# Attention over channels with a gated FFN on one core: k's norms spread by transposes and DMAs, and a new order for scalings, G/H tiles and one load of v

## The chip, the cores and the metric

The kernel runs on one core of a Trainium2 chip. TensorE multiplies matrices, VectorE, ScalarE and GpSimd work on elements, SyncE (SP) only issues DMAs. The metric is the time of one execution in microseconds on the device, the median of several runs; lower is better.

## The reference

```python
B, N, C = (4, 6016, 256)

def _attn_ref(q, k, v, tau):
    qn = q / (np.linalg.norm(q, axis=1, keepdims=True) + 1e-06)
    kn = k / (np.linalg.norm(k, axis=1, keepdims=True) + 1e-06)
    s = kn.transpose(0, 2, 1) @ qn / tau
    s = s - s.max(-1, keepdims=True)
    a = np.exp(s)
    a /= a.sum(-1, keepdims=True) + 1e-09
    return (v @ a).astype(np.float32)

def _moe_ref(x, w_gate, w_val, w_out):       # 24064 tokens, 256 -> 1536 -> 256
    gate = 1.0 / (1.0 + np.exp(-(x @ w_gate)))
    val = x @ w_val
    return (gate * val @ w_out).astype(np.float32)
```

The result is `_moe_ref` of the attention output, its four batches put one after another, with tau 1.0. q and k are normalised over the rows, one norm for each of the 256 channels, so the attention matrix is only 256 x 256 for each batch.

## The kernel before

**The algebra.** Since the attention output is v times a 256 x 256 matrix a, the kernel never forms it. For each batch it makes G = a w_gate and H = a w_val (256 x 1536 each, from the exponentials `e`, the weights and the row sums), and the GLU then works on v directly: `ps_gate` from G and the transposed v (`vT`), `ps_val` from H and vT. ScalarE takes tanh of half the gate (L518), VectorE forms (tanh + 1) times val in `hT` (L519). The output product with w_out is done as seven products of half-size blocks, for which VectorE makes operand sums of hT (`a_sum`, L541) and GpSimd, once, sums of w_out (`w_sums`, L215); sums of the products are put together by ScalarE copies (L595, L602) and GpSimd additions (L596 to L613).

**The tiling.** A batch has 47 row tiles of 128, in 12 chunks: eleven of four tiles and one of three (`NCH`, `groups`). A chunk has 12 slots, f = 0 to 11, one for each 128 of the 1536 hidden channels (`glu(b, ci, f)`). So a batch has 144 slots, numbered here from 0; slot 108 is chunk 9, f = 0. In each slot the order of the program is: the GLU block (two ps_gate and two ps_val matmuls), a twelfth of the output products of the chunk before (`run_work`), perhaps an operand sum, and then the side work listed for that slot. Operand sums come at f = 1, 3, 4, 5, 6 for the chunk before (`NEXT_SLOTS`) and at f = 7 to 11 for the chunk itself (`OWN_SLOTS`); f = 0 and 2 have none. The order on each engine is that of the program, written out by hand.

**Side work.** `side_work(b)` (L749 to L806) prepares batch n = b + 1 while batch b's GLU runs. It spreads over the first 96 slots the loads of q and k, the scores (`ps_s`, in the one-bank pool `pss`) and the squares for the norms. With s0 = 98 it then lists: the folding of the squares, the norm matmuls, an inverse root (GpSimd, L355 to L359) giving the four columns `r` for q and k, their reciprocals on VectorE at slot 108 (`norms_inv`), `spread_both` at slot 110, `copy_rk` at 111, the two scalings of the scores at 112 (`scale_x`, VectorE), the exponentials at 113 and 114 (`exps`, ScalarE), the row sums at 116 (`all_sums`), and the twelve G/H tiles (`gh`) at 117 + 9 i // 4, from 117 to 141, in turn in `pss` and in the other one-bank pool, `psm`. A tile with row block 0 is stored by ScalarE (L464), one with row block 1 by VectorE (L466).

**k's norms.** A scaling needs the q norm of a channel on each partition, which `r` has, and k's norms along the free axis on every partition, which it has not. `spread_both` makes this with TensorE: two fp32 matmuls of a broadcast column of `r` with the identity give `ps_rk` in PSUM, and ScalarE copies it to `rk_sb`. Batch 0 uses `spread_k` and `weights` instead, ahead of the GLU. `sums_start` opens the row-sum bank with a matmul of one row of ones with a row of eps (L413), and `row_sums` adds the sums of e to it.

**Queues.** GpSimd issues all loads of q, k, v and the weights[...]; at the start it issues batch 0's q and k, v's chunk 0, the weights of G and H in four pieces each (256, 256, 512, 512 columns), v's chunk 1, and w_out. Later v loads go two chunks ahead, at f = 0. SP issues the transpose of each v chunk (`transpose_v`, L483, listed at f = 2 of the chunk before; batch 0's chunk 0 goes through TensorE instead) and the stores of the output (L654, listed at f = 4). A DMA on SP waits for its data, and all behind it on SP wait with it.

Of the kernel before, what the change touches and what calls it, by code (L numbers as in the profile page):

```python
# [9 lines left out]
FP32 = mybir.dt.float32  # L10
BF16 = mybir.dt.bfloat16
# [42 lines left out]
def kernel(  # L54
# [20 lines left out]
    nc = tc.nc  # L75
    P = nc.NUM_PARTITIONS
# [4 lines left out]
    B, N, C = q.shape  # L81
    CW, DFF = moe_w_gate.shape
    assert CW == C and C % P == 0 and N % P == 0 and DFF % P == 0
    NT = N // P
    CB = C // P
    FC = DFF // P
# [4 lines left out]
    NCH = (NT + TPC - 1) // TPC  # L91
# [5 lines left out]
    def rows(x, b):  # L97
        return x[b].rearrange("(p t) c -> p t c", p=P)
# [3 lines left out]
    def pool(name, bufs, **kw):  # L102
        return ctx.enter_context(tc.tile_pool(name=name, bufs=bufs, **kw))

    consts = pool("consts", 1)
# [3 lines left out]
    attp = pool("attp", 1)  # L109
# [5 lines left out]
    spool = pool("spool", 1)  # L115
    mpool = pool("mpool", 2)
    opool = pool("opool", 2)
    psg = pool("psg", 2, space=PSUM)
    psv = pool("psv", 2, space=PSUM)
    pso = pool("pso", 2, space=PSUM)  # L120
    pss = pool("pss", 1, space=PSUM)
    psm = pool("psm", 1, space=PSUM)
# [3 lines left out]
    def mm(out, lhsT, rhs, start, stop, **kw):  # L126
        nc.tensor.matmul(out, lhsT=lhsT, rhs=rhs, start=start, stop=stop, **kw)  # L127
# [16 lines left out]
    def load_v(b, ci):  # L144
        t0, nt = groups[ci]
        v_sb = vpool.tile([P, TPC, C], BF16, tag="v", name="v_sb")
        nc.gpsimd.dma_start(out=v_sb[:, :nt, :], in_=rows(v, b)[:, t0 : t0 + nt, :])
        vs[b, ci] = v_sb
# [16 lines left out]
    ident_f = consts.tile([P, P], FP32)  # L165
    make_identity(nc, ident_f)
    ones_bf = consts.tile([P, P], BF16)
# [3 lines left out]
    one_two = consts.tile([P, 2], BF16)  # L171
    nc.vector.memset(one_two[:, 0:1], 1.0)
    nc.vector.memset(one_two[:, 1:2], 2.0)
    ones_row = consts.tile([1, P], BF16)
    nc.vector.memset(ones_row, 1.0)
    eps_row = consts.tile([1, CB, 2], BF16)
    nc.vector.memset(eps_row[:, :, 0:1], 1e-9)
    nc.vector.memset(eps_row[:, :, 1:2], 2e-9)
    shift = consts.tile([P, 1], FP32)
    nc.vector.memset(shift, -inv_tau)  # L180

# [8 lines left out]
    w_out_sb = consts.tile([P, FC, C], BF16)  # L190
    pieces = [(0, FG // 2), (FG // 2, FG // 2)] + [(fg * FG, FG) for fg in range(1, NFG)]
    for f0, nf in pieces:
        for w, src in enumerate((moe_w_gate, moe_w_val)):
            nc.gpsimd.dma_start(  # L194
                out=w_sb[w][f0 // FG][:, :, ds(f0 % FG, nf)],
                in_=src.rearrange("(t p) f -> p t f", p=P)[:, :, ds(f0, nf)],
            )
    load_v(0, 1)

    w_sums = consts.tile([P, len(B_SUMS), FC // 2, P], BF16)  # L200
    w_f32 = {}
# [1 line left out]
    for n in range(FC // TPC):  # L203
        w_f32[n] = f32pool.tile([P, TPC, C], FP32, tag="f32", name="w_f32")
        nc.gpsimd.dma_start(
            out=w_f32[n], in_=moe_w_out.rearrange("(t p) c -> p t c", p=P)[:, n * TPC : (n + 1) * TPC, :]
# [16 lines left out]
    st = {}  # L223
# [85 lines left out]
        )  # L309

    def spread_both(b):
        s = st[b]
        s["rk_ps"] = psm.tile([P, C], FP32, tag="m", name="ps_rk")
        for i in range(CB):
            mm(
                s["rk_ps"][:, ds(i * P, P)],
                s["r"][:, CB + i : CB + i + 1].to_broadcast([P, P]),
                ident_f,
                True,
                True,  # L320
            )

    def copy_rk(b):
        s = st[b]
        s["rk_sb"] = attp.tile([P, C], FP32, tag="rk", name="rk_sb")
        nc.scalar.copy(s["rk_sb"], s["rk_ps"])

    def norms_sqrt(b):
        s = st[b]
# [18 lines left out]
    def root_steps(b):  # L348

        s = st[b]  # L350
        x, y = s["sq_n"], s["y"]
        t = attp.tile([P, 2 * CB], FP32, tag="tn", name="t_n")
        s["r"] = attp.tile([P, 2 * CB], FP32, tag="r", name="r")
        for _ in range(3):
            nc.gpsimd.tensor_tensor(out=t, in0=x, in1=y, op=ALU.mult)  # L355
            nc.gpsimd.tensor_tensor(out=t, in0=t, in1=y, op=ALU.mult)
            nc.gpsimd.tensor_scalar(out=t, in0=t, scalar1=-0.5, scalar2=1.5, op0=ALU.mult, op1=ALU.add)
            nc.gpsimd.tensor_tensor(out=y, in0=y, in1=t, op=ALU.mult)
        nc.gpsimd.tensor_tensor(out=s["r"], in0=x, in1=y, op=ALU.mult)  # L359
# [50 lines left out]
    def sums_start(b, ni, pl, tag):  # L410

        ps_r = pl.tile([P, ni, 2], FP32, tag=tag, name="ps_r")
        mm(ps_r, ones_row, eps_row[:, :ni, :], start=True, stop=False, skip_group_check=True)  # L413
        return ps_r

    def row_sums(b, i0, ps_r):
# [224 lines left out]
    def run_work(work, share):  # L641

        upto = sum(w[0] for w in work) * share
        done = 0
        while work and done < upto:
            cost, fn, *args = work.pop(0)
            fn(*args)
            done += cost

    def store():  # L650
        while stores:
            b, ci = stores.pop(0)
            t0, nt = groups[ci]
            nc.sync.dma_start(out=out_rows[b][:, t0 : t0 + nt, :], in_=ffn.pop((b, ci))[:, :nt, :])  # L654
# [91 lines left out]
    gh(0, gh_first[3], pso, "o")  # L746


    def side_work(b):  # L749


        side = {}

        def at(slot, fn, *a):
            side.setdefault(divmod(slot, FC), []).append((fn, a))

        for ci in range(NCH):
            nb, nci = (b, ci + 1) if ci + 1 < NCH else (b + 1, 0)
            lb, lci = (b, ci + 2) if ci + 2 < NCH else (b + 1, ci + 2 - NCH)
            if nb < B:  # L760
                at(ci * FC + 2, transpose_v, nb, nci)
            if lb < B:
                at(ci * FC + 0, load_v, lb, lci)
            if (b, ci) == (0, 0):
                for i in range(FC // TPC):
                    at(8, copy_w_out, i)
                for n, m in enumerate((1, 0, 3, 2, 4)):
                    for i in range(FC // TPC):
                        at(10 + 2 * n, sum_w_out, m, i)
        n = b + 1  # L770
        if n == B:
            return side
        first, last = (14 if b == 0 else 0), 8 * FC
        for g, (t0, nt) in enumerate(groups):
            s0 = first + g * (last - first) // NCH
            if b == 0:
                at(max(0, s0 - 12), load_qk, n, t0, nt)
            elif s0 >= 24:
                at(s0 - 24, load_qk, n, t0, nt)
            for u in range(nt):  # L780
                at(first + (t0 + u) * (last - first) // NT, score, n, t0, u)
            if g == 0:
                at(s0, acc_start, n)
            for i, (fn, w) in enumerate(((acc_square, 0), (acc_add, 0), (acc_square, 1), (acc_add, 1))):
                at(s0 + 1 + 2 * i, fn, n, g, w)
        if n + 1 < B:
            for g, (t0, nt) in enumerate(groups[:3]):
                at(NCH * FC - 24 + 8 * g, load_qk, n + 1, t0, nt)
        s0 = 8 * FC + 2
        at(s0 if b == 0 else s0 - 2, acc_fold, n, 0)  # L790
        at(s0 + 1 if b == 0 else s0, acc_fold, n, 1)
        at(s0 + 3, norms_mm, n)
        at(s0 + 4, root_seed, n)
        at(s0 + 4, root_steps, n)
        at(s0 + 10, norms_inv, n)
        at(s0 + 12, spread_both, n)
        at(s0 + 13, copy_rk, n)
        at(s0 + 14, scale_x, n, 0)
        at(s0 + 14, scale_x, n, 1)
        at(s0 + 15, exps, n, 0)  # L800
        at(s0 + 16, exps, n, 1)
        at(s0 + 18, all_sums, n)
        at(s0 + 18, gh_tiles, n)
        for i, piece in enumerate(gh_order):
            at(s0 + 19 + 9 * i // 4, gh, n, piece, *((pss, "s"), (psm, "m"))[i % 2])
        return side  # L806


# [5 lines left out]
    def gh_piece(n):  # L814
        gh(0, gh_first[n], *gh_banks[n % 4])

    prev = None
    for b in range(B):
        side = side_work(b)
        for ci in range(NCH):  # L820
            final = (b, ci) == (B - 1, NCH - 1)
            for f in range(FC):
                mid = gh_mid.get(f) if (b, ci) == (0, 0) else None
                glu(b, ci, f, None if mid is None else (lambda: gh_piece(mid)))
                if prev is not None:
                    if f == 4:
                        store()
                    if f + final in NEXT_SLOTS and prev != (0, 0):
                        a_sum(*prev, 1, NEXT_SLOTS[f + final])
                    run_work(work, 1 / max(1, FC - final - f))  # L830
                if f in OWN_SLOTS and not final and (b, ci) != (0, 0):
                    a_sum(b, ci, 0, OWN_SLOTS[f])
                for fn, a in side.get((ci, f), ()):
                    fn(*a)
                if (b, ci) == (0, 0):
                    for i in gh_end.get(f, ()):
                        gh_piece(i)
            prev = (b, ci)
            if not final:
                work = out_work(*prev)  # L840
# [39 lines left out]
```

## Time and profile before

| what | value |
|---|---|
| median of 4 runs | 806.28 us (806.17 to 806.32) |
| time of the profiled execution | 805.97 us |
| its span in the trace | 804.2 us |
| mean granted TensorE clock | 0.997 |
| first ps_gate matmul of chunk 0, of chunk 1 (batch 0) | 36.67 us, 52.64 us |
| VectorE's product L519, 128x512, mean | 682 ns, x528 |
| operand sum L541, 128x768, mean | 621 ns, x430 |
| G/H store, 128x512: VectorE L466, ScalarE L464 | 744 ns, 688 ns |
| scaling L302, 128x256 | 470 ns, x6 |
| vT transpose on SP, issue to landing, median | 3.9 us, x47 |
| output store of 512 KB on SP, issue to landing, median | 3.4 us, x43 |

The span runs from the first to the last instruction in the trace; the time of that execution is 1.8 us more, for what lies around it. A mean is that of one instruction by itself; instructions of one engine overlap a little at their ends, so the distance between two starts is shorter than the mean (0.60 for L519, 0.47 for L541). A matmul's start is well known and its end is modelled, so TensorE's time is best read from one start to the next.

### The profile page before, as it was taken

The numbers are of one execution on the slowest core, as the hardware profiler recorded it, in microseconds if no ns is written. First come the engines' busy times: TensorE is split into PE (matmuls) and PEld (weight loads), VectorE is DVE, ScalarE is ACT, GpSimd is POOL, SyncE is SP. The second block draws the span as 40 slices with busy tenths as digits, with TensorE's granted clock in tenths as the row PEclk, the third lists the DMA queues.
The fourth block names the chain that finished last, engine by engine and source line by source line (L and its number), as shares of the span: only waits on it lengthen the run. The fifth ranks groups of instructions, "written<-read, shape, count | busy, mean of one in ns | idle before, by whom it ended". The sixth has DMA issues, their size and how long they took to land.

```text
span 804.2 us, 17852 instructions
## 1 busy us (share of the span) xinstructions
PE 783.9 (97%) x6745; PEld 499.0 (62%) x6745; DVE 707.1 (88%) x1213; ACT 525.9 (65%) x890; POOL 355.7 (44%) x568
## 2 busy tenths in 40 slices
PE   3899999999999999999999999999999999999998
PEld 2546666666666666666666666666656666666666
DVE  5767999999879999999887999999988898898996
ACT  3767777766667776775666767776666565666664
POOL 4573545435552454335443544443534244444433
PEclk9999999999999999999999999999999999999999
DMA  9998758532567457422467476524222422433402
GB/s 215 205 197 124 127 94 136 100 67 46 106 125 130 86 108 140 86 53 55 89 121 127 80 138 112 106 54 91 61 54 55 89 62 68 83 62 70 83 28 73
DMA packets 78918, 78.48 MB, mean 98 GB/s; under 512 B 51824, under 2 KB 56688, under 8 KB 78832
## 3 DMA queue, kind: packets, MB, share of 16 engines
q0 software_dynamic: 22192, 39.59, 30.2%
q1 hardware_dynamic: 56064, 36.91, 20.7%
q8 instruction: 52, 0.85, 0.4%
q10 hardware_dynamic: 576, 0.85, 0.3%
q14 instruction: 34, 0.28, 0.1%
HBM read 78.64 MB, written 24.64 MB: 128 GB/s over the span
## 4 chain that ended last, share of the span: by engine, by line
PE 92%; DMA 5%; POOL 1%; DVE 1%; issue 0%; POOLq 0%
PE ps_val L127 29%; PE ps_gate L127 29%; PE ps_o L127 27%; PE ps_s L127 4%; DMA k_sb<-in_k_dram 3%; PE ps_gh L127 2%; DMA vT<-v_sb 1%; DMA v_sb<-in_v_dram 1%; DVE hT L519 0%; POOL w_gate L194 0%; POOL w_val L194 0%; DVE acc L284 0%; DVE sums L541 0%; PE ps_rk L127 0%; PE ps_end L127 0%
## 5 line engine op out<-in xcount | busy, mean ns | idle before, releaser
L518 ACT ACTIVATE g_sb<-ps_gate 128x512 f32<-128x512 f32 (+1 forms) x576 | 338.4, 588 | 223.6 <-PE ps_gate L127 214.5
L519 DVE SCALAR_TENSOR_TENSOR hT<-g_sb,ps_val 128x512 bf16<-128x512 f32 (+1 forms) x576 | 385.3, 671 | 78.8 <-ACT g_sb L518 69.7
L127 PE MATMUL ps_gate<-vT,gh_G 128*128 128x512 bf16 (+1 forms) x1152 | 337.6, 375 | 0.8 <-DMA vT<-v_sb 0.8
L127 PE MATMUL ps_val<-vT,gh_H 128*128 128x512 bf16 (+1 forms) x1152 | 337.7, 375 | 0.3 <-DVE hT L519 0.3
L541 DVE TENSOR_TENSOR sums<-hT 128x768 bf16<-128x768 bf16 (+1 forms) x460 | 277.6, 604 | 0.0
L127 PEld LDWEIGHTS <-sums 128*128 128x128 bf16 x2670 | 183.0, 98 | 82.1 <-DVE sums L541 0.5
L127 PEld LDWEIGHTS <-gh_H 128*128 128x128 bf16 x1152 | 112.7, 98 | 131.6 <-DVE gh_H L466 0.8
L612 POOL TENSOR_TENSOR out_sb<-out_sb,m_sb 128x256 f32<-128x256 f32 x89 | 78.5, 882 | 234.9 <-ACT out_sb L602 206.4
L127 PE MATMUL ps_o<-w_sums,sums 128*128 128x128 bf16 x1602 | 154.4, 219 | 0.0
L127 PEld LDWEIGHTS <-hT 128*128 128x128 bf16 x1200 | 88.3, 98 | 46.8
L596 POOL TENSOR_TENSOR m_sb<-m_sb 128x128 f32<-128x128 f32 x89 | 42.7, 479 | 158.8 <-ACT m_sb L595 158.7
L127 PEld LDWEIGHTS <-gh_G 128*128 128x128 bf16 x1152 | 96.9, 98 | 15.9 <-DMA vT<-v_sb 1.3
L127 PE MATMUL ps_o<-w_out_sb,sums 128*128 128x128 bf16 x1068 | 96.2, 219 | 0.0
L127 PE MATMUL ps_o<-w_sums,hT 128*128 128x128 bf16 x1068 | 95.5, 219 | 0.0
L127 PE MATMUL ps_s<-k_sb,q_sb 128*128 128x256 bf16 x376 | 68.5, 283 | 15.6 <-DMA k_sb<-in_k_dram 8.9
L613 POOL TENSOR_TENSOR out_sb<-out_sb 128x256 f32<-128x256 f32 x89 | 76.6, 861 | 7.0
L602 ACT COPY out_sb<-ps_o 128x512 f32<-128x512 f32 x89 | 52.2, 587 | 11.9 <-PE ps_o L127 9.2
L284 DVE TENSOR_TENSOR acc<-acc,sq 128x1024 bf16<-128x1024 bf16 (+1 forms) x66 | 59.8, 906 | 0.0
L597 POOL TENSOR_TENSOR m_sb<-m_sb 128x128 f32<-128x128 f32 x89 | 52.6, 591 | 7.0
L246 ACT ACTIVATE sq<-k_sb 128x1024 bf16<-128x1024 bf16 (+2 forms) x44 | 44.8, 1027 | 12.1 <-DMA k_sb<-in_k_dram 12.0
L127 PEld LDWEIGHTS <-q_sb 128*128 128x128 bf16 x376 | 32.5, 101 | 21.1 <-issue 10.7
L595 ACT COPY m_sb<-ps_o 128x384 f32<-128x384 f32 x89 | 42.6, 479 | 3.4 <-PE ps_o L127 0.6
(84 smaller groups left out, 309.3 us busy)
## 6 DMA issues: line engine op xcount, KB each, us to landing
out_dram<-out_sb SPq DMA_DIRECT2D x43, 512.0 KB, 3.4
v_sb<-in_v_dram POOLq DMA_DIRECT2D x44, 256.0 KB, 5.2
q_sb<-in_q_dram POOLq DMA_DIRECT2D x35, 256.0 KB, 6.0
k_sb<-in_k_dram POOLq DMA_DIRECT2D x35, 256.0 KB, 7.4
q_sb<-in_q_dram POOLq DMA_DIRECT2D x4, 512.0 KB, 11.4
k_sb<-in_k_dram POOLq DMA_DIRECT2D x4, 512.0 KB, 13.4
w_f<-in_moe_w_out_dram POOLq DMA_DIRECT2D x3, 512.0 KB, 9.2
out_dram<-out_sb SPq DMA_DIRECT2D x3, 384.0 KB, 2.8
```

Of the source, the lines that this page charges most:

```text
L127: nc.tensor.matmul(out, lhsT=lhsT, rhs=rhs, start=start, stop=stop, **kw)
L246: nc.scalar.activation(out=sq[:, :nt, :], in_=src[:, :nt, :], func=ACT.Square)
L284: nc.vector.tensor_tensor(out=acc[:, :nt, :], in0=acc[:, :nt, :], in1=st[b]["sq", w][:, :nt, :], op=ALU.add)
L518: nc.scalar.activation(out=g_sb[:, :n], in_=ps_gate[:, :n], func=ACT.Tanh, scale=0.5)
L519: nc.vector.scalar_tensor_tensor(out=hts[b, ci][:, f, :n], in0=g_sb[:, :n], scalar=1.0, in1=ps_val[:, :n], op0=ALU.add, op1=ALU.mult,)
L541: nc.vector.tensor_tensor(out=sums[b, ci, g][:, m, :, : half * P], in0=hT[:, f0 + k0 : f1 : 2, ds(r0 * half * P, half * P)], in1=hT[:, f0 ...
L595: nc.scalar.copy(m, states[p]["ps"][:, : 3 * P].rearrange("p (n c) -> p n c", c=P))
L596: nc.gpsimd.tensor_tensor(out=m[:, 1, :], in0=m[:, 1, :], in1=m[:, 2, :], op=ALU.add)
L597: nc.gpsimd.tensor_tensor(out=m[:, 2, :], in0=m[:, 1, :], in1=m[:, 0, :], op=ALU.add)
L602: nc.scalar.copy(o[:, p : p + half + 1 : half, :], states[p]["ps"].rearrange("p (t c) -> p t c", c=C),)
L612: add(out=ends, in0=ends, in1=states[p]["m"][:, 1:3, :], op=ALU.add)
L613: add(out=ends, in0=ends, in1=mids, op=ALU.subtract)
```

## The change

Five things change.

1. `spread_both` no longer uses TensorE. `r` of batches 1 to 3 is now the first four columns of `r_wide`, a 128 x 32 tile that starts as zeros. VectorE transposes it in blocks of 32 x 32 to `rT`, SP writes k's two rows of 128 norms to a row in DRAM (a new pool, `dpool`), and reads the row back to all 128 partitions as `rk_sb`. `copy_rk` is gone. All is listed at slot 108, with the reciprocals.
2. The scalings go to slots 120 and 122, the exponentials to 123 and 124, the row sums to 126.
3. The twelve G/H tiles go to slots 127, 129, ... 149; those past 143, tiles 9 to 11, are done in slots 1, 3 and 5 of the next batch (`spill`), all in `psm`.
4. `sums_start` opens the bank with 128 rows of ones and of eps / 128 in place of one row; the constants change with it. This holds for batch 0 too.
5. At the start, v's chunk 1 is loaded ahead of the last pieces of w_gate and w_val in place of after them.

```diff
-    ones_row = consts.tile([1, P], BF16)
-    nc.vector.memset(ones_row, 1.0)
-    eps_row = consts.tile([1, CB, 2], BF16)
-    nc.vector.memset(eps_row[:, :, 0:1], 1e-9)
-    nc.vector.memset(eps_row[:, :, 1:2], 2e-9)
+    eps_two = consts.tile([P, CB, 2], BF16)
+    nc.vector.memset(eps_two[:, :, 0:1], 1e-9 / P)
+    nc.vector.memset(eps_two[:, :, 1:2], 2e-9 / P)
+    r_wide = consts.tile([P, 32], FP32)
+    nc.vector.memset(r_wide, 0.0)
...
     for f0, nf in pieces:
+        if f0 + nf == DFF:
+            load_v(0, 1)
         for w, src in enumerate((moe_w_gate, moe_w_val)):
...
-    load_v(0, 1)
...
     def spread_both(b):
-        s = st[b]
-        s["rk_ps"] = psm.tile([P, C], FP32, tag="m", name="ps_rk")
+
+        s = st[b]
+        rT = attp.tile([P, 32], FP32, tag="rT", name="rT")
+        nc.vector.transpose(out=rT, in_=r_wide)
+        row = dpool.tile([C], FP32, tag="row", name="row")
         for i in range(CB):
-            mm(
-                s["rk_ps"][:, ds(i * P, P)],
-                s["r"][:, CB + i : CB + i + 1].to_broadcast([P, P]),
-                ident_f,
-                True,
-                True,
-            )
-
-    def copy_rk(b):
-        s = st[b]
+            nc.sync.dma_start(
+                out=row[ds(i * P, P)].rearrange("(s j) -> s j", j=32), in_=rT[CB + i : P : 32, :]
+            )
         s["rk_sb"] = attp.tile([P, C], FP32, tag="rk", name="rk_sb")
-        nc.scalar.copy(s["rk_sb"], s["rk_ps"])
+        nc.sync.dma_start(out=s["rk_sb"], in_=row.rearrange("(o c) -> o c", o=1).to_broadcast([P, C]))
...
-        s["r"] = attp.tile([P, 2 * CB], FP32, tag="r", name="r")
+        s["r"] = r_wide[:, : 2 * CB]
...
-        mm(ps_r, ones_row, eps_row[:, :ni, :], start=True, stop=False, skip_group_check=True)
+        mm(ps_r, ones_bf, eps_two[:, :ni, :], start=True, stop=False, skip_group_check=True)
...
         at(s0 + 10, norms_inv, n)
-        at(s0 + 12, spread_both, n)
-        at(s0 + 13, copy_rk, n)
-        at(s0 + 14, scale_x, n, 0)
-        at(s0 + 14, scale_x, n, 1)
-        at(s0 + 15, exps, n, 0)
-        at(s0 + 16, exps, n, 1)
-        at(s0 + 18, all_sums, n)
-        at(s0 + 18, gh_tiles, n)
+        at(s0 + 10, spread_both, n)
+        at(s0 + 22, scale_x, n, 0)
+        at(s0 + 24, scale_x, n, 1)
+        at(s0 + 25, exps, n, 0)
+        at(s0 + 26, exps, n, 1)
+        at(s0 + 28, all_sums, n)
+        at(s0 + 28, gh_tiles, n)
         for i, piece in enumerate(gh_order):
-            at(s0 + 19 + 9 * i // 4, gh, n, piece, *((pss, "s"), (psm, "m"))[i % 2])
+            slot = s0 + 29 + 2 * i
+            if slot < NCH * FC:
+                at(slot, gh, n, piece, *((pss, "s"), (psm, "m"))[i % 2])
+            else:
+                spill.setdefault((n, *divmod(slot - NCH * FC, FC)), []).append((gh, (n, piece, psm, "m")))
...
-                for fn, a in side.get((ci, f), ()):
+                for fn, a in spill.get((b, ci, f), []) + side.get((ci, f), []):
                     fn(*a)
```

More of the change, by code (lines that the diff above doesn't have):

```diff
@@ L117 @@
     opool = pool("opool", 2)
+    dpool = pool("dpool", 1, space=bass.MemoryType.DRAM)
     psg = pool("psg", 2, space=PSUM)
@@ L746 @@
     gh(0, gh_first[3], pso, "o")
+    spill = {}
     def side_work(b):
```

## The prediction

> **What bounds the kernel now.** I read the engine totals first, then who waited for whom, then TensorE's instructions in order of time around the edited places, then the SP queue.
>
> ```profile
> PE 783.9 (97%) x6745; PEld 499.0 (62%) x6745; DVE 707.1 (88%) x1213; ACT 525.9 (65%) x890; POOL 355.7 (44%) x568
> ```
>
> TensorE is busy for 97% of the span, VectorE for 88%. The totals do not say whether VectorE ever holds TensorE up; the waits of TensorE do (us in total, times, longest):
>
> ```profile
> PE ps_s L127 <- DMA k_sb<-in_k_dram: 8.9, 6, 3.1
> PE ps_s L127 <- ACT k_sb L183: 6.7, 1, 6.7
> PE ps_gate L127 <- DMA vT<-v_sb: 0.8, 1, 0.8
> PE ps_r L127 <- ACT e_sb L398: 0.6, 1, 0.6
> PE ps_val L127 <- DVE hT L519: 0.3, 1, 0.3
> ```
>
> The first, second and fourth lie in the first 36 us, before the GLU begins. The third is batch 0's chunk 1, at 52.64. After that VectorE stops TensorE once, near 102. I added up TensorE's starts from 52 us on against its own cadence (two 512-column matmuls 0.43, a 128-column one 0.056): beside that 0.47 and a 0.11 near 168, the only gaps over 0.06 are at the row sums of the three later batches. So a slot of the planner (one GLU block with its share of the output products, 1.25 us) is TensorE's, and **a change is worth what it takes off TensorE's own list, plus 0.94 us of waiting**; VectorE's load matters only if it grows past its cover.
>
> **TensorE loses the spread of k's norms (removed).** In order of time on TensorE, batch 1:
>
> ```profile
> 188.12 0.33 PE L127 MATMUL ps_o<-w_sums,sums 128*128 128x128 bf16 x3
> 188.29 0.66 PE L127 MATMUL ps_rk<-ident_f,r 128*128 128x128 f32 x4
> 188.79 0.59 PE L127 MATMUL ps_gate<-vT,gh_G 128*128 128x512 bf16 x2
> ```
>
> The columns are start, length, work. From the start of ps_rk to the next start is 188.79 - 188.29 = 0.50 us, and the chain shows 0.50 at 381.87 and 575.29 too. Three batches: **-1.50 us**. The ScalarE copy of it (L326, 0.38) goes as well; ScalarE is at 65% and holds nobody, so that counts nothing.
>
> **The row sums' first matmul loses its one-row shape.**
>
> ```profile
> 196.15 0.33 PE L127 MATMUL ps_o<-w_out_sb,sums 128*128 128x128 bf16 x3
> 196.41 0.17 PE L127 MATMUL ps_r<-eps_row,ones_row 1*128 1x4 bf16 x1
> 196.52 0.25 PE L127 MATMUL ps_r<-one_two,e_sb 128*128 128x2 bf16 x4
> 196.63 0.59 PE L127 MATMUL ps_gate<-vT,gh_G 128*128 128x512 bf16 x2
> ```
>
> Three products need 3 x 0.056 = 0.17, so the one-row matmul could start at 196.32 and starts at 196.41: 0.09 lost. It then holds TensorE 0.11, while its four full-height neighbours with two columns take 0.11 together, 0.03 each: 0.08 more. The other two batches show 0.09 + 0.08 and 0.10 + 0.07. With ones_bf (128 rows) it should cost what its neighbours cost: 0.17 less, three times, **-0.51 us**. Here a rule speaks against the change. The Trainium skill (TensorE: Matmul & The Clock Gate, LDWEIGHTS) has a weight load cost its columns and not its contraction rows, so that going from 1 to 128 rows changes nothing: 0 by the rule. Another page (TensorEngine Tiling (Array Packing), Key Properties) says that a change of tiling mode drains the array, which would explain a gap on both sides. The row has the gap three times of three, so I take 0.51 and keep 0 as the other end.
>
> **v's second chunk goes ahead of the last two weight pieces (moved).** The chain that ended last, early on:
>
> ```profile
> 33.39 0.71 POOL w_gate L194
> 34.10 0.68 POOL w_val L194
> 34.77 8.36 DMA v_sb<-in_v_dram
> 43.15 9.44 DMA vT<-v_sb
> 52.59 0.05 issue
> 52.64 0.60 PE ps_gate L127 x2
> ```
>
> The last ps_val pair of chunk 0 starts at 51.27 and holds TensorE until 51.27 + 0.43 = 51.70; chunk 1 starts at 52.64, when its transposed v is there: 0.94 lost. Loads issued by GpSimd land in order: the gate piece ahead of the last two at 31.98 + 6.0 = 38.0, its val at 32.67 + 6.6 = 39.3, the last gate at 33.38 + 7.2 = 40.6, the last val at 34.07 + 7.8 = 41.9, v at 34.77 + 8.36 = 43.1: one per 1.3 us. Moved up two places, v lands near 40.5. Its transpose took 9.44 under full DMA load and meets the same load, so it lands at 40.5 + 9.44 = 49.9, which is 1.8 ahead of 51.70: **-0.94 us**. The ends: 0 if it takes 11.2 or more up to 52.6 (the next transpose took 12.3, but that one began behind the first on its queue); 0.94 is all that can be had. The two weight pieces land 1.3 us later, at 41.9 and 43.1. Their first readers are the matmuls at 43.05 (gate) and 45.63 (val), so 1.1 and 2.5 us of cover; without it TensorE would pay the lateness one to one. The loads of w_out behind them keep their place; v's transpose now shares the engines with them earlier. Their last cast ends at 48.7, and their first reader comes at about 52.6.
>
> **What SP gets (added and moved past).** At slot 108 three small DMAs enter SP's list: two rows of 512 B to DRAM, then a 128 KB broadcast back, which waits for both to land. Behind them stand the transpose for chunk 10 and a store. Before, in batch 1:
>
> ```profile
> 178.00 1.24 SPq L483 DMA_TRANSPOSE vT<-v_sb  x1
> 188.26 0.33 SPq L654 DMA_DIRECT2D out_dram<-out_sb  x1
> ```
>
> SP runs ahead of TensorE: the transpose went at 178.00, and TensorE wants it at slot 120, 184.53 + 12 x 1.255 = 199.6. Now it waits for VectorE's reciprocal, which ended at 187.05. The trace has no VectorE transpose; its ends are 0.15 (128x4, L363) and 0.29 (128x128 f32 copy, L676); I take 0.3. Nor has it so small a DMA: the nearest rows are 64 KB stores on SP and ACT that landed in 1.6 and 1.5, and a 128 KB store in 2.0. So: SP issues at 187.4 and 187.7 (0.33 each), both rows are down at 189.3, the broadcast is issued at 189.4 and lands at 191.4, the transpose goes at 189.7 and lands, by its own 3.1 there, at 192.8. **That is 6.8 us ahead of 199.6**: 0. As ends, a fixed 2 us per DMA, as the skill's page DMA: Bandwidth & Descriptors (Anatomy of one DMA) states for the GpSimd path, would add 0.4 to the first hop; the slowest transpose after 100 us took 8.9, which would land at 198.6 and still be in time. The store behind moves from 188.26 to about 191; its buffer is next written in chunk 10's last third. scale_x reads the broadcast at slot 120, on VectorE near 201: 9 us of cover. It stands on VectorE ahead of the GLU products, so late data there would stop TensorE.
>
> **Scalings, exponentials and G/H tiles move.** The two scalings (0.43 each) go from one slot with an operand sum to two slots without; nothing waited before, so 0. The twelve G/H tiles keep their two matmuls (0.43 for both), and six go on VectorE at 0.67. Their slots with a VectorE store (f = 1, 5, 9) all carry a sum: 0.60 + 0.47 + 0.67 = 1.74 against 1.25 + 0.43 = 1.68 for TensorE in that slot, then the other three slots of four at 1.07 against 1.25 or more; two PSUM buffers bridge 0.06. Taken as 0. Every sum stretched to 1.00, as some are beside GpSimd, would make it the 0.47 seen near 101. One tight place: tile 8 uses the score bank at slot 143, and the next batch's scores begin in that bank at slot 144. By the rows there, ScalarE would end its store at 234.48 and TensorE wants the bank at 234.74: 0.26 of cover, at two batch borders; if gone, a few tenths. The last tile, in the next batch's slot 5, is read at slot 8. The changed memsets lie in VectorE's 4.0 us wait for the first q: 0.
>
> **The sum.** 1.50 + 0.51 + 0.94 = 2.95. The span goes from 804.2 to 801.25, the profiled execution's time from 805.97 to 803.02. The median of the runs is 0.31 above that execution, so the forecast is 806.28 - 2.95 = **803.3 us**.
>
> **Rivals.**
> - One-row matmul costs the same (the rule): 803.8. For it, the rule; against it, three rows alike.
> - v's transpose stays late, or the last gate piece misses 43.05: 803.3 + 0.94 = 804.3. For it, DMA is full until 52 us and the transpose now shares with more weights; against it, in-order landings with steps of 1.3 to 1.5 us even beside the transpose.
> - VectorE becomes the bound in the moved tiles' slots: 18 stores, six of them costing the 0.47 seen near 101, is 2.8 and makes 806.1, no change. For it, VectorE at 88%; against it, no wait of TensorE now in slots with the same load.
> - **Slower: the spread stops SP's transpose.** Place: slot 108 of each batch. Its two hops are 3.9 us (187.4 to landing, twice about 2.0). Cover ends at 3.9 + 6.8 = 10.7, and each us beyond costs 3 us in three batches; from 11.7 on it eats the whole gain. With 7.4 for each hop, the median of a k load, 14.8 - 10.7 = 4.1, times 3 is 12.3: 815.6. Against it, DMA engines idle for long stretches there.
>
> **How the numbers follow.** Forecast 0.50, one-row rival 0.13, v's rival 0.17, VectorE 0.11, SP 0.09. This kernel can be told from no change at 0.2%, 1.6 us. The first three lie beyond it (804.3 is 2.0 below): faster 0.80; VectorE's is the same, 0.11; SP's slower, 0.09. The range begins at 802.5, where the 0.47 and 0.11 gaps also close (802.7) with a little more, and runs to 805.6, which takes in v's rival with no gain at the row sums (804.8) and part of VectorE's, leaving out SP's and the rest.
>
> **What will show it.** Right: no ps_rk matmul after 40 us; row sums of 0.14 instead of 0.31; chunk 1 starting 0.43 after chunk 0's last ps_val pair; no wait of TensorE for vT or hT in chunks 9 to 11. Wrong: x_sb waiting for a DMA, scores waiting for gh_G, ps_gh waiting for the last w_gate.

## The result and the profile after

The changed kernel takes 804.83 us (median of 35 runs, 804.24 to 806.92) against 806.24 (53 runs): a ratio of 0.9983, interval 0.9978 to 0.9987, or 1.41 us less. The forecast was 803.3, so a little under half of the expected 2.95 us came. The profiled execution took 804.85 with a span of 803.1, against 805.97 and 804.2.

The engine totals of the changed kernel are nearly the same, and the waits of TensorE (us in total, times, longest) show what did not happen:

```profile
PE 783.4 (98%) x6733; PEld 498.4 (62%) x6733; DVE 712.5 (89%) x1216; ACT 525.6 (65%) x887; POOL 356.3 (44%) x568
```

```profile
PE ps_s L128 <- DMA k_sb<-in_k_dram: 7.1, 5, 2.2
...
PE ps_gate L128 <- DMA vT<-v_sb: 1.4, 1, 1.4
...
PE ps_r L128 <- ACT e_sb L396: 0.7, 1, 0.7
...
PE ps_val L128 <- DVE hT L517: 0.3, 1, 0.3
```

The wait for vT, which was to go, grew from 0.8 to 1.4. From 55 us on TensorE waits for no score, no G/H tile and no vT, and VectorE nowhere for `rk_sb`; the one wait for hT is the old one, near 102.

Because TensorE hardly ever pauses, the starts of its GLU blocks can be set side by side, block by block, in the two traces. This table is worked out so (start after less start before, us):

| block (slot of which batch) | difference | since the row above |
|---|---|---|
| batch 0, slot 0 | -0.12 | |
| batch 0, slot 12 (chunk 1) | +0.44 | +0.56: the wait for vT is 1.52, was 0.94 |
| batch 0, slot 108 | +0.44 | 0 |
| batch 1, slot 6 | -0.30 | -0.74 |
| batch 2, slot 6 | -1.04 | -0.74 |
| batch 3, slot 6 | -1.78 | -0.74 |
| batch 3, slot 138 | -1.79 | 0 |
| end of the span | -1.14 | +0.65: the end is longer |

Each border between batches is worth 0.74, together 2.2: more than the 2.01 of the forecast. The rest was lost at two places, at the start (0.56 in this execution in place of a gain of 0.94) and, unforeseen, at the very end (0.65).

The row sums of batch 1, in order of time on TensorE, now take 208.93 - 208.81 = 0.12:

```profile
208.75 0.22 PE L128 MATMUL ps_o<-w_sums,sums 128*128 128x128 bf16 x1
208.81 0.17 PE L128 MATMUL ps_r<-eps_two,ones_bf 128*128 128x4 bf16 x1
208.83 0.24 PE L128 MATMUL ps_r<-one_two,e_sb 128*128 128x2 bf16 x4
208.93 0.59 PE L128 MATMUL ps_gate<-vT,gh_G 128*128 128x512 bf16 x2
```

The full-height matmul that opens the bank costs 0.02; the whole group took 0.31 before. And the chain that ended last, early in the changed kernel (start, length, what):

```profile
33.25 7.62 DMA v_sb<-in_v_dram
40.87 0.02 issue
40.88 12.14 DMA vT<-v_sb
53.03 0.05 issue
53.08 0.61 PE ps_gate L128 x2
```

v did land 2.3 us earlier, at 40.87 as the forecast had it (40.5). Its transpose then took 12.14 in place of 9.44, and landed later than before.

### The profile page after: what moved, and what is told of

It is laid out like the page before. It is cut to its first block, busy times and chain, and to the rows that moved or that the text cites. A ratio compares the mean times of both kernels' runs of the same rounds, so it can differ in the third digit from the quotient of the medians.

```text
span 803.1 us, 17845 instructions
## 1 busy us (share of the span) xinstructions
PE 783.4 (98%) x6733; PEld 498.4 (62%) x6733; DVE 712.5 (89%) x1216; ACT 525.6 (65%) x887; POOL 356.3 (44%) x568
## 4 chain that ended last, share of the span: by engine, by line
PE 92%; DMA 6%; DVE 1%; POOL 1%; issue 0%; POOLq 0%
PE ps_val L128 29%; PE ps_gate L128 29%; PE ps_o L128 27%; PE ps_s L128 4%; DMA k_sb<-in_k_dram 3%; PE ps_gh L128 2%; DMA vT<-v_sb 2%; DMA v_sb<-in_v_dram 1%; DVE hT L517 0%; DVE acc L286 0%; DVE sums L539 0%; POOL w_gate L197 0%; POOL w_val L197 0%; PE ps_end L128 0%; POOL q_sb L138 0%
## 5 line engine op out<-in xcount | busy, mean ns | idle before, releaser
L539 DVE TENSOR_TENSOR sums<-hT 128x768 bf16<-128x768 bf16 (+1 forms) x460 | 281.6, 612 | 0.0
L128 PE MATMUL ps_s<-k_sb,q_sb 128*128 128x256 bf16 x376 | 70.4, 291 | 13.6 <-DMA k_sb<-in_k_dram 7.1
```

What stands on the lines that cost most here:

```text
L539: nc.vector.tensor_tensor(out=sums[b, ci, g][:, m, :, : half * P], in0=hT[:, f0 + k0 : f1 : 2, ds(r0 * half * P, half * P)], in1=hT[:, f0 ...
```

## The experiments

For each run, "the kernel before" is the one timed beside it on the same chip (806.31 to 806.35). Where the interval of a run's ratio overlaps that of the changed kernel (0.9978 to 0.9987), as for v_back, v_earlier, one_row and te_spread, the time alone does not tell the two apart, and the starts of the blocks carry the reading.

### v's load: moved back, moved alone, moved further, and a shorter queue

**Moved back** (run v_back).

```diff
     for f0, nf in pieces:
-        if f0 + nf == DFF:
-            load_v(0, 1)
         for w, src in enumerate((moe_w_gate, moe_w_val)):
...
+    load_v(0, 1)
```

> The changed kernel with v's chunk 1 loaded behind all weight pieces again. Theory (the transpose of v's chunk 1 cannot end before GpSimd's queue of loads is empty, so the move gains nothing and the earlier start only stretches it): chunk 1 starts at 52.6 +- 0.2 us as before, 0.4 ahead of the changed kernel's 53.08, and the time is 0.3 to 0.6 us below the changed kernel's 804.83, near 804.4. Rival (the 53.08 is chance, from one execution to another; the move gains as forecast): the time is some 0.9 us above the changed kernel's, near 805.7.

Measured: 804.53 us, ratio 0.9978 (0.9969 to 0.9986), 0.30 below the changed kernel. Chunk 1 starts at 52.87, just past the 52.6 +- 0.2 expected; the wait is 1.24 us.

**Moved alone** (run v_alone), in the kernel before.

```diff
     for f0, nf in pieces:
+        if f0 + nf == DFF:
+            load_v(0, 1)
         for w, src in enumerate((moe_w_gate, moe_w_val)):
...
-    load_v(0, 1)
```

> The kernel before with only the load of v's chunk 1 moved ahead of the last two weight pieces. Theory (empty queue decides): chunk 1 starts at 53.0 +- 0.2 in place of 52.64, the last end of that transpose comes within 1 us after the last of the q and k loads issued near 40 us has landed, and the time is 806.24 + 0.4, near 806.6. Rival (the move gains its 0.94): 805.3.

Measured: 806.71 beside 806.34, ratio 1.0004 (0.9996 to 1.0012). Chunk 1 starts at 53.45 (expected 53.0 +- 0.2), 0.81 later than before; 0.19 of that is there from slot 0 on, so the wait is 0.94 + 0.62 = 1.56. All later blocks keep the 0.81. By time alone this is not told from no change; by the trace the rival's gain is not there.

**Moved two places further up** (run v_earlier).

```diff
-        if f0 + nf == DFF:
+        if f0 == FG:
             load_v(0, 1)
```

> The changed kernel with v's chunk 1 loaded two places further up, ahead of the weight pieces of columns 512 to 1023 too, so that it lands about 2.6 us earlier, near 38.3. Theory (empty queue decides): its transpose is stretched again and lands at 53 +- 0.4; chunk 1 starts near 53.1, the time stays at 804.8 +- 0.4, or is above it where a weight piece comes late for chunk 0. Rival (the transpose takes a fixed 12.1 us under full load, whenever it starts): it lands near 50.4, chunk 1 starts without a wait 0.43 after chunk 0's last ps_val pair, and the time falls by up to 1.5, to 803.3.

Measured: 805.41, ratio 0.9989 (0.9980 to 0.9997). The same chain in this kernel:

```profile
32.09 6.25 DMA v_sb<-in_v_dram
38.33 0.02 issue
38.35 15.48 DMA vT<-v_sb
53.83 0.05 issue
53.88 0.60 PE ps_gate L128 x2
```

This settles it: v lands at 38.33, and its transpose takes 15.48 and lands later still. A fixed duration under load (12.1) is out. The expectation was a landing at 53 +- 0.4, so 53.83 is past its edge: an earlier start is not only useless, it costs.

The cost of the first move is small beside the spread of single executions. From chunk 0's first ps_gate to chunk 1's, the six kernels here that load v last take 15.97 to 16.33 us, 16.18 in the mean; the five that load it two places earlier, with the q and k loads where they were, take 16.23 to 16.83, 16.53 in the mean; this one takes 17.10.

**A shorter queue** (run late_qk). Batch 1's first q and k loads go behind the casts of w_out.

```diff
-        first, last = (14 if b == 0 else 0), 8 * FC
+        first, last = (17 if b == 0 else 0), 8 * FC
...
-                at(max(0, s0 - 12), load_qk, n, t0, nt)
+                at(max(8, s0 - 12), load_qk, n, t0, nt)
```

> The changed kernel with batch 1's first q and k loads put behind the casts of w_out (slot 8 in place of slots 2), and its scores and squares spread over slots 17 to 95 in place of 14 to 95. The queue of loads is then empty when v's chunk 2 has landed, near 49.6. Theory (empty queue decides): the transpose of chunk 1 lands at 50 to 51, chunk 1 starts without a wait, and the time falls by about 1.5 us to 803.3, less what the denser side work may cost VectorE near 94 to 102 us (there 0 to 1 us). Rival (a fixed 12.1 us under load): chunk 1 still starts near 53.1 and the time stays within 0.4 of 804.8.

Measured: 803.33 us, ratio 0.9961 (0.9949 to 0.9974), 1.50 below the changed kernel and 3.0 below the kernel before; it beats both. In order of time on TensorE:

```profile
51.27 0.59 PE L128 MATMUL ps_val<-vT,gh_H 128*128 128x512 bf16 x2
51.70 0.59 PE L128 MATMUL ps_gate<-vT,gh_G 128*128 128x512 bf16 x2
52.13 0.59 PE L128 MATMUL ps_val<-vT,gh_H 128*128 128x512 bf16 x2
```

Chunk 1's ps_gate follows chunk 0's last ps_val pair after 0.43; the wait is gone. The q and k loads are now issued at 49.22 and 49.76, in place of 40.18 and 41.40. v was loaded at the same place as in the changed kernel, so **what held the transpose was the loads issued beside and after it, not the time at which its data came**. The denser side work cost no more than before: the VectorE stop near 102 became one of 0.41 near 121.

### The row sums' shape, and the spread on TensorE

**One row again** (run one_row).

```diff
-    eps_two = consts.tile([P, CB, 2], BF16)
-    nc.vector.memset(eps_two[:, :, 0:1], 1e-9 / P)
-    nc.vector.memset(eps_two[:, :, 1:2], 2e-9 / P)
+    ones_row = consts.tile([1, P], BF16)
+    nc.vector.memset(ones_row, 1.0)
+    eps_row = consts.tile([1, CB, 2], BF16)
+    nc.vector.memset(eps_row[:, :, 0:1], 1e-9)
+    nc.vector.memset(eps_row[:, :, 1:2], 2e-9)
...
-        mm(ps_r, ones_bf, eps_two[:, :ni, :], start=True, stop=False, skip_group_check=True)
+        mm(ps_r, ones_row, eps_row[:, :ni, :], start=True, stop=False, skip_group_check=True)
```

> The changed kernel with the row sums opened by one row of ones and eps again. By the trace of before (gaps of 0.09 and 0.08 around the one-row matmul in each of three batches): 0.5 to 0.6 us more than the changed kernel, 805.4; the row sums take 0.32 of TensorE's time in each batch in place of 0.12. By the rule that a weight load costs its columns and not its rows: no difference, 804.8 +- 0.2.

Measured: 805.47, ratio 0.9990 (0.9982 to 0.9998), 0.64 above the changed kernel. From chunk 1 to batch 3 the blocks gain 1.68 on the kernel before, where the changed kernel gains 2.23: 0.55, or 0.18 for each batch. In batch 1:

```profile
209.26 0.22 PE L128 MATMUL ps_o<-w_sums,sums 128*128 128x128 bf16 x1
209.41 0.17 PE L128 MATMUL ps_r<-eps_row,ones_row 1*128 1x4 bf16 x1
209.52 0.25 PE L128 MATMUL ps_r<-one_two,e_sb 128*128 128x2 bf16 x4
209.63 0.59 PE L128 MATMUL ps_gate<-vT,gh_G 128*128 128x512 bf16 x2
```

The one product before it needs 0.06, so TensorE could go on at 209.32; it starts at 209.41 and the group ends at 209.63: 0.31 again, in a new place with other neighbours. The measurement decides for the gap and against no difference.

**The spread on TensorE** (run te_spread).

```diff
-        nc.vector.transpose(out=rT, in_=r_wide)
...
         for i in range(CB):
-            nc.sync.dma_start(
-                out=row[ds(i * P, P)].rearrange("(s j) -> s j", j=32), in_=rT[CB + i : P : 32, :]
-            )
+            mm(
+                s["rk_ps"][:, ds(i * P, P)],
+                s["r"][:, CB + i : CB + i + 1].to_broadcast([P, P]),
+                ident_f,
+                True,
+                True,
+            )
...
-        at(s0 + 10, spread_both, n)
+        at(s0 + 12, spread_both, n)
+        at(s0 + 13, copy_rk, n)
```

> The changed kernel with k's norms spread by TensorE and copied by ScalarE again (slots 110 and 111), all else as changed. Step of the forecast: TensorE pays 0.50 us in each of three batches again; the starts of ps_gate fall back by 1.5 us against the changed kernel. On the end of the span there are two theories. If the spread's small DMAs lengthen the end (from the last store's issue on ACT to the span's end: 2.70 us in the kernel before, 3.1 to 3.5 in four kernels with the DMAs), it is 2.7 again and the time is 804.83 + 1.5 - 0.6 = 805.7. If the longer end is chance or comes from something else of the change, it stays near 3.3 and the time is 806.3.

Measured: 805.81, ratio 0.9994 (0.9986 to 1.0002), 0.98 above the changed kernel. The blocks gain 0.72 from chunk 1 to batch 3 in place of 2.23: 1.51, as reckoned. But the time is only 0.98 worse: the end of the span (from the last store's issue, below) is 2.71 again.

### Were the later slots needed?

Run old_slots:

```diff
-        at(s0 + 22, scale_x, n, 0)
-        at(s0 + 24, scale_x, n, 1)
+        at(s0 + 14, scale_x, n, 0)
+        at(s0 + 14, scale_x, n, 1)
...
-            slot = s0 + 29 + 2 * i
+            at(s0 + 19 + 9 * i // 4, gh, n, piece, *((pss, "s"), (psm, "m"))[i % 2])
```

(The exponentials and row sums go back to their old slots too.)

> The changed kernel with scalings, exponentials, row sums and G/H tiles back in the slots of before (112 to 141), while k's norms still come by DMA. In the changed kernel's trace the broadcast lands at about 193.4, 386.3 and 580.6, and the scalings of slot 112 would be wanted at about 192.4, 385.1 and 577.8. Theory (the later slots are what makes the DMA path free): VectorE waits 1.0, 1.2 and 2.8 us for rk_sb, TensorE loses most of that, 2 to 5 us in all, and the time is 807 to 810. Rival (VectorE's slack covers it): 804.8 +- 0.5.

Measured: 810.26, ratio 1.0048 (1.0035 to 1.0062), 5.4 above the changed kernel and just past the 807 to 810 expected. Waits of this kernel:

```profile
DVE x_sb L304 <- DMA rk_sb<-row: 4.8, 3, 2.4
PE ps_val L128 <- DVE hT L517: 4.3, 4, 2.1
```

VectorE waits three times for `rk_sb`, and TensorE then waits nearly as long for VectorE. So the later slots, which this run takes back all together, are not a gain of their own: they are the price of the DMA path, and without them the change would be slower than the kernel before.

### The end of the span

In the changed kernel the last store, of 64 KB, is issued on ACT's queue at 799.71 and the span ends 3.36 later; before, 801.50 and 2.70. What SP waits for at the end, before and after:

```profile
SPq L875 <- DMA out_dram<-end: 0.9, 2, 0.6
```

```profile
SPq L878 <- DMA out_dram<-end: 1.7, 2, 1.4
```

In the changed kernel SP waits longer for the last stores to land. Four runs add parts of the spread, idle, to the kernel before; the first, idle_dmas, adds all of it.

```diff
+    def idle_dmas(b):
+        rT = attp.tile([P, 32], FP32, tag="rT", name="rT")
+        nc.vector.transpose(out=rT, in_=r_wide)
+        row = dpool.tile([C], FP32, tag="row", name="row")
+        for i in range(CB):
+            nc.sync.dma_start(
+                out=row[ds(i * P, P)].rearrange("(s j) -> s j", j=32), in_=rT[CB + i : P : 32, :]
+            )
+        spare = attp.tile([P, C], FP32, tag="spare", name="spare")
+        nc.sync.dma_start(out=spare, in_=row.rearrange("(o c) -> o c", o=1).to_broadcast([P, C]))
...
+        at(s0 + 10, idle_dmas, n)
         at(s0 + 12, spread_both, n)
```

> The kernel before, to which the spread's VectorE transpose, two row stores and broadcast load are added at slot 108 of each batch; nobody reads what they bring, and TensorE spreads the norms as before. If these DMAs lengthen the end: TensorE's starts stay as before within 0.1, the end from the last store's issue on ACT is 3.1 to 3.5 us in place of 2.70, and the time is 806.24 + 0.4 to 0.8, near 806.9. If not: 806.3 +- 0.2 and an end of 2.7.

Measured: 806.89 beside 806.31, ratio 1.0007 (0.9999 to 1.0015); the end is 3.12. Then the row stores alone (idle_rows):

```diff
-        spare = attp.tile([P, C], FP32, tag="spare", name="spare")
-        nc.sync.dma_start(out=spare, in_=row.rearrange("(o c) -> o c", o=1).to_broadcast([P, C]))
```

> The kernel before, to which only the VectorE transpose and the two 512-byte row stores (4 partitions each) are added at slot 108; no broadcast load, and nobody reads the row. With all three DMAs the end of the span (from the last store's issue on ACT) was 3.08 us, without them 2.70. If the stores from four partitions are what lengthens the end: 3.0 to 3.5, and the time is 806.3 + 0.3 to 0.6. If the broadcast does it: 2.7, and 806.3 +- 0.2.

And the broadcast alone, of a row of q, with no transpose and no row store (idle_bcast):

```diff
+        nc.sync.dma_start(out=spare, in_=q[0][0:1, :].to_broadcast([P, C]))
```

> The kernel before, to which only a broadcast load of one 1 KB row to 128 partitions (from an input, read by nobody) is added at slot 108. If the stores from four partitions lengthen the end of the span: it stays 2.7 and the time 806.3 +- 0.2. If the broadcast does it: 3.0 to 3.5, and 806.3 + 0.3 to 0.6.

Measured: row stores 806.81 beside 806.35 (1.0005, 0.9997 to 1.0014), end 3.15; broadcast 806.32 (1.0000, 0.9991 to 1.0008), end 2.69. And with the stores into a row of the output, without a DRAM tile (idle_out):

```diff
-        row = dpool.tile([C], FP32, tag="row", name="row")
+        row = out[(B - 1) * N, :]
```

> The kernel before with the VectorE transpose and the two 512-byte row stores at slot 108, as in the run with the row stores alone (end of the span 3.10 in place of 2.70), but into a row of the output that batch 3 overwrites later, so that the program has no DRAM tile of its own. If the stores themselves lengthen the end: 3.0 to 3.5 again, time 806.35 + 0.4. If it is the DRAM tile: 2.7, time 806.35 +- 0.2.

Measured: 806.71 beside 806.35 (1.0005, 0.9996 to 1.0013), end 3.17.

From the last store's issue to the span's end, in all profiled runs (the expectations took it from spans rounded to 0.1 us, so their figures differ by up to 0.05):

| kernel | row stores on SP | end, us |
|---|---|---|
| before, v_alone, te_spread, idle_bcast | no | 2.70, 2.69, 2.71, 2.69 |
| after, v_back, v_earlier, late_qk, one_row, old_slots | yes | 3.36, 3.47, 3.10, 3.35, 3.17, 3.05 |
| idle_dmas, idle_rows, idle_out, even_rows (below) | yes | 3.12, 3.15, 3.17, 3.16 |

The two groups do not touch. Small stores on SP, the last of them over 200 us before, come with 0.4 to 0.8 us more at the end, wherever they write to; the broadcast does not. The four idle runs' intervals by time all reach 1; it is the split of the ends that carries this.

How it comes about stays open. It is not always the wait for the last stores: in idle_rows, idle_out and even_rows SP waits for them 0.9 or 1.0 in all and 0.6 at the longest, as before. And something else splits the kernels in just the same way. Of the DMA queues between the last store's issue and the end, the changed kernel has one that the kernel before has not (packets, MB, share of the 16 DMA engines):

```profile
q14 instruction: 1, 0.01, 1.3%
```

All ten kernels with the longer end have one packet of this queue in that stretch, and none of the four others has. So the row stores may lengthen the end only by the instructions that they add to the program, which would move a load of instructions into the end. No run separates the two.

**Other stores, which failed** (run even_rows). On the kernel with the late q and k loads:

```diff
-        rT = attp.tile([P, 32], FP32, tag="rT", name="rT")
-        nc.vector.transpose(out=rT, in_=r_wide)
         row = dpool.tile([C], FP32, tag="row", name="row")
-        for i in range(CB):
-            nc.sync.dma_start(
-                out=row[ds(i * P, P)].rearrange("(s j) -> s j", j=32), in_=rT[CB + i : P : 32, :]
-            )
+        nc.sync.dma_start(out=row.rearrange("(i p) -> p i", p=P), in_=s["r"][:, CB : 2 * CB])
```

> The changed kernel with batch 1's first q and k loads late, as in the run that gave 803.33, and with k's norms written to the DRAM row by one DMA of 128 partitions, two floats each, without the transpose on VectorE. If stores from four partitions lengthen the end of the span, it is 2.7 in place of 3.33 and the time is 803.33 - 0.6 = 802.7. If any of these small DMAs does, it stays at 3.1 to 3.5 and the time at 803.3 +- 0.2. TensorE's starts are the same in both; 256 elements of 4 bytes may take longer to land, with 6 us of cover for the transpose behind them.

Measured: 810.75, ratio 1.0051 (1.0037 to 1.0064), and the end stays long. SP in batch 1, and the waits of TensorE:

```profile
185.99 0.38 SPq L317 DMA_DIRECT2D row<-r_wide  x1
195.28 0.33 SPq L319 DMA_DIRECT2D rk_sb<-row  x1
195.72 2.02 SPq L476 DMA_TRANSPOSE vT<-v_sb  x1
```

```profile
PE ps_gate L128 <- DMA vT<-v_sb: 5.5, 3, 2.7
```

One store of 256 scattered floats holds SP for 195.28 - 185.99 = 9.3 us, and the transpose behind it comes late in all three batches. The 6 us of cover in the expectation were too few. This is the prediction's slower rival come true, by a store of another layout.

## Why the prediction was right, and where not

**The spread leaves TensorE: right.** The runs with and without differ by 1.51 over three batches, forecast 1.50. On SP all came as described, a little later: in batch 1 of the changed kernel

```profile
187.76 1.18 SPq L320 DMA_DIRECT2D row<-rT  x2
190.01 0.33 SPq L324 DMA_DIRECT2D rk_sb<-row  x1
190.46 1.31 SPq L481 DMA_TRANSPOSE vT<-v_sb  x1
```

the broadcast is issued at 190.01 (forecast 189.4) and the transpose at 190.46 (189.7). The broadcast's landing was the term most under-sized: 3.2 to 3.7 us for 2.0 taken from a store. The cover of 9 us took it up; the VectorE transpose took 0.21, between the two ends given.

**The row sums: right.** 0.18 to 0.19 for each batch, forecast 0.17. The forecast took the row over the rule in the Trainium skill (TensorE: Matmul & The Clock Gate, LDWEIGHTS) that a weight load costs its columns alone. The rule is on the load; here the group of one-row and full-height matmuls lost 0.18 to 0.19 each time. That fits the sentence on draining in the skill's page TensorEngine Tiling (Array Packing), Key Properties, but no run shows that the one-row matmul changes the tiling mode. The 0.05 still missing to 0.74 for each border is a short stall of the kernel before in slot 2 of the next batch (six products there took 0.39 where they need 0.33); it is gone with the G/H tile in slot 1, and old_slots, which has no tile there, still takes 0.39.

**v's move: this step failed.** The sum took a transpose of 9.44 and let it begin earlier "under the same load". Its landing follows the queue of loads instead. It comes just after the last of the loads issued up to 42 us, a k load: at 52.59 after 51.72 before, at 53.03 after 52.32 in the changed kernel, at 53.83 after 53.60 with v moved further. So the sooner it begins, the longer it takes (9.4, 12.1 and 15.5 for starts at 43.2, 40.9 and 38.4). The ends given, 0 to -0.94, left out a loss, and the move cost 0.3 to 0.4 (804.53 against 804.83 with it undone, 806.71 against 806.34 with it alone, and 0.35 between the means of the starts). The v rival held the right outcome and half of the reason: DMA is full until 52 us. The trace of before had this sign already (41.11 + 10.6 = 51.7 for that k load).

**Scalings, exponentials, tiles: right** that nothing waits for them in the new slots. What was costed at 0 as a change of its own is needed by the spread, as 810.26 shows. The score bank's narrow cover held: no wait of the scores for a tile.

**The end was in no step.** It takes 0.4 to 0.8 us more in the kernels with the row stores, for a cause that stays open. With it the account closes: 2.2 gained at the borders, less 0.3 to 0.4 at the start, less 0.4 to 0.8 at the end, leaves 1.0 to 1.5; 1.41 was measured.

That the time still fell inside the range is in part luck. The range made room for v's gain to be missing, but for no loss there and for nothing at the end; the room left for the row sums and for VectorE, which both went right, took these up.

## What to carry to other kernels

When a transfer is late, look at what else is in flight until it lands before moving its start: here moving it forward cost time, and holding two later loads back gained 1.50 us. Work that leaves the bounding engine for DMAs needs its readers moved by the length of the new path, and a dependent pair of DMAs on a queue holds all behind it, so the layout of even a 1 KB store matters. The end of the program can change with edits far away, as it did here with nothing late on TensorE, so set the traces side by side up to the last line.

## What the runs showed of the hardware

- A DMA transpose beside a filled queue of loads took 9.4, 12.1 and 15.5 us, the more the earlier it began, with the 16 DMA engines full (share 1.11, 1.17 and 1.11 in those stretches); it took 3.1 in batch 1 of the kernel before, at a share of 0.46.
- 1 KB stored to DRAM as eight pieces of 128 bytes let SP issue the broadcast that reads it after 2.1 to 3.8 us in the changed kernel; stored as 256 single floats, after 8.2 to 9.3.
- In the run with the scattered floats TensorE stood still 2.8 us near 587, and afterwards ran slower for about 4 us. Busy time by stretch (span, then PE, PEld, DVE, ACT and POOL busy with instructions, granted clock, DMA share, GB/s):

```profile
580.00:586.00 6.00, 6.00 (x56) 3.76 (x55) 5.70 (x10) 3.57 (x6) 2.85 (x4) 1.00 0.36 24
586.00:589.90 3.90, 1.24 (x12) 0.71 (x11) 2.35 (x5) 1.18 (x2) 1.95 (x3) 1.00 1.01 181
589.90:593.90 4.00, 4.00 (x20) 2.19 (x21) 1.24 (x3) 1.20 (x2) 0.34 (x1) 0.57 1.06 283
593.90:600.00 6.10, 6.10 (x55) 3.74 (x53) 5.55 (x10) 4.26 (x9) 1.56 (x3) 1.00 0.27 51
```

  The granted clock is 0.57 in the mean of those 4 us and 1.00 again behind them; pairs of 512 columns take 0.85 in place of 0.43. That stall cost 2.8 for itself and 1.7 more in the two slots behind it; stalls of 1.9 and 1.2 in the other two batches cost nothing more.
